# Seven block products in place of eight for the second network's gate and value projections

## The chip, the cores and the metric

The kernel runs on one core of a Trainium2 chip. The core has five engines with a queue each: TensorE (PE in the profile, with its weight loads as PEld), VectorE (DVE), ScalarE (ACT), GpSimd (POOL) and SyncE (SP), which here only issues DMAs. Each engine works through its instructions in their order and waits on semaphores for the others. The metric is the device time of one execution in microseconds: a median of 1072.18 us over three runs (1070.48 to 1072.44).

## The reference, cut to what matters

Linear attention over 4 x 8 heads of 576 positions feeds two dense networks, one after the other, on 2304 tokens of width 512. All values are float32.

```python
x = attention(q, k, v, w_phi)          # [2304, 512] after the heads are joined
h = x @ w_in                           # first network: 512 -> 2048
x = (np.maximum(h, 0.0) ** 2) @ w_out  # 2048 -> 512
gate = 1.0 / (1.0 + np.exp(-(x @ w_gate)))   # second network: 512 -> 1536
val = x @ w_val                              # 512 -> 1536
out = (gate * val) @ w_out2                  # 1536 -> 512
```

## The kernel before, in words

Every matmul operand is kept as two float32r tiles, the rounded value ("hi") and what is left of it ("lo"). A product of two operands is three matmuls, hi x hi, hi x lo and lo x hi (`passes`, L45), summed in PSUM. So each weight tile must be split before use: `wsplit` (L121) takes a raw 128 x 512 float32 tile `wf`, copies hi on ACT (L124) and subtracts lo on DVE or POOL (L125) into a tile `hl`, of which there are six.

The program has three stages: attention, the first network in steps `h_step` and `o_step`, and the second network in steps `gv_step` and `o2_step`. During attention and the first network, `converts` brings every weight into its final form (`weight`, L97 to L110) and parks it in DRAM; a fetch on SP's queue brings it back as `wf` before each use (ten buffers), so that each weight is fetched and split again for every token block.

The second network takes the 2304 tokens in four blocks of 512 and a last one of 256, and for each block the 1536 hidden units in 12 chunks of 128. The step of one chunk (`gv_step`, L536): `project` (L459) makes the gate's 12 matmuls (four contraction tiles, three passes) and the value's 12, each of 512 columns, into one PSUM bank each; ACT takes the sigmoid (L540), DVE multiplies (L541), `g_split` makes the operand `g` (cast on DVE L93, subtraction on DVE L94). `o2_step` (L556) adds the chunk's 12 matmuls into the four banks that hold the block's output, one step later. At the end of a block the banks are copied out in halves by ACT (L575) and DVE (L573). At the start of a block `xsplit` makes hi and lo of its tokens, the tiles `xs`.

PSUM has eight banks, all of one pool (`bank`). The order on each engine comes from a scheduler that runs when the program is built: it puts instructions in the order of the code's priorities as far as its own estimate of when their operands and buffers are free allows, so an engine's order is fixed before the program runs and can interleave two steps.

Of the kernel before, what the change touches and what calls it, by code (L numbers as in the profile page):

```python
# [9 lines left out]
F32 = mybir.dt.float32  # L10
# [9 lines left out]
def attention_moe_moe2(ctx, tc, q, k, v, w_phi, w_in, w_out, w_gate, w_val, w_out2, out):  # L20
    nc = tc.nc
# [35 lines left out]
    def bank(n):  # L57
        return ps.tile([P, 512], F32, tag="a", name="a")[:, :n]
# [72 lines left out]

    def w2_src(n):
        c, o = divmod(n, 3)
        return row_src(w_out2, c) if o == 2 else col_src(w_val if o else w_gate, c)

    nblk = len(blocks)
    ng = len(GROUPS)
# [4 lines left out]


    def pieces_of(s):
        if s < ns1:
            t, c = divmod(s, C1)
            return [((t, 2 * c), 2 * c)], ((t, 2 * c + 1), 2 * c + 1)
        t, c = divmod(s - ns1, C2)
        return [((ng + t, 3 * c + o), NW1 + 3 * c + o) for o in range(2)], ((ng + t, 3 * c + 2), NW1 + 3 * c + 2)

    ahead = 2
    fetched = {}

    def fetch_for(s):
        if s < ns1 + ns2:
            ins, out = pieces_of(s)
            for key, n in [*ins, out]:
                t = wf.tile([P, NJ * P], F32, tag="wf", name="wf")
                nc.sync.dma_start(out=t, in_=parked[n])
                fetched[key] = t  # L160

    def split_in(s):
        if s < ns1 + ns2:
            for key, n in pieces_of(s)[0]:
                if key not in ws:
                    wsplit(key, fetched.pop(key), nc.gpsimd if s < C1 else nc.vector)

    def split_out(s):
        key, n = pieces_of(s)[1]
        wsplit(key, fetched.pop(key), nc.gpsimd if s < ns1 else nc.vector)  # L170

    with ExitStack() as actx:
        cst = actx.enter_context(tc.tile_pool(name="cst", bufs=1))
# [270 lines left out]
                split_in(0)  # L444

    gp = ctx.enter_context(tc.tile_pool(name="gp", bufs=2, reuse_waits="tile"))

    gs = {}
    ys = {}
    last_g = [None]  # L450

    def convert(n):
        park(n, weight(wpa, w1_src(n) if n < NW1 else w2_src(n - NW1)))

    def xsplit(key, t, c0, n):
        for j in range(NJ):
            xsplit_j(key, t, c0, n, j, nc.scalar)

    def project(w, key, t, n):  # L459
        pp = bank(n)  # L460
        k = 0
        for j in range(NJ):
            for x, y in passes:
                nc.tensor.matmul(pp, lhsT=w[:, x, j, :], rhs=xs[key, t, j][:, y, :], start=k == 0, stop=k == 3 * NJ - 1)  # L464
                k += 1
        return pp

    def g_split(key, r):
        g = gp.tile([P, 2, r.shape[1]], F32R, tag="g", name="g", bufs=3)
        last_g[0] = split(g, r)  # L470
        gs[key] = g

    def h_step(g, c):
        w = ws.pop((g, 2 * c))
        for t in GROUPS[g]:
            n = sizes[t]
            pp = project(w, 1, t, n)
            r = gp.tile([P, n], F32, tag="r", name="r")
# [41 lines left out]
    fetch_for(1)  # L520
    for s in range(ns1 + 1):
        if s < ns1:
            t, c = divmod(s, C1)
            if c == 0 and t:
                for u in GROUPS[t]:
                    xsplit(1, u, *blocks[u])
            fetch_for(s + ahead)
            h_step(t, c)
            split_out(s)
            split_in(s + 1)  # L530
        if s >= 1:
            o_step(*divmod(s - 1, C1))
        if s < ns1:
            converts(s)

    def gv_step(t, c):  # L536
        n = sizes2[t]
        pt = [project(ws.pop((ng + t, 3 * c + o)), 2, t, n) for o in range(2)]
        r = gp.tile([P, n], F32, tag="r", name="r2")
        nc.scalar.activation(r, pt[0], AF.Sigmoid)  # L540
        nc.vector.tensor_tensor(r, pt[1], r, ALU.mult)  # L541
        g_split((2, t, c), r)

    def pieces(c0, n):
        c = c0
        while c < c0 + n:
# [9 lines left out]
    def o2_step(t, c):  # L556
        ntt = sizes2[t] // P
        if c == 0:
            os_[t] = [bank(512) for u in range(ntt)]
        w = ws.pop((ng + t, 3 * c + 2))  # L560
        g = gs.pop((2, t, c))
        for u in range(ntt):
            for n, (x, y) in enumerate(passes):
                nc.tensor.matmul(os_[t][u], lhsT=g[:, x, u * P:(u + 1) * P],  # L564
                                 rhs=w[:, y].rearrange("p j f -> p (j f)"),
                                 start=c == 0 and n == 0, stop=c == C2 - 1 and n == 2)
        if c == C2 - 1:
            for u in range(ntt):
                o = gp.tile([P, DM], F32, tag="o", name="osb", bufs=4)
# [9 lines left out]
    done = 0  # L579
    for s in range(ns2 + 2):  # L580
        if s < ns2:
            t, c = divmod(s, C2)
            if c == 0:
                xsplit(2, t, *blocks2[t])
            fetch_for(ns1 + s + ahead)
            gv_step(t, c)
            split_out(ns1 + s)
            split_in(ns1 + s + 1)

        while done < ns2 and done <= s - (1 if s < ns2 - 1 else 2):  # L590
            o2_step(*divmod(done, C2))
            done += 1


# [28 lines left out]
```

## Time and profile before

| what | us |
|---|---|
| median of three runs | 1072.18 |
| the profiled execution's own time | 1071.14 |
| its span, first to last instruction | 1069.3 |
| PE busy | 1052.0 (98%) |
| DVE busy | 705.8 (66%) |
| ACT busy | 516.2 (48%) |
| POOL busy | 218.3 (20%) |

The profiled execution is one run of the program; its own time is 1.84 us above its span, for what lies around the span. Busy time counts the instructions of an engine. Matmuls overlap each other, so the distance between starts, and not the length of one, tells what a matmul costs; the chain in order of time gives these distances.

### The profile page before, as it was taken

How to read it: one execution, taken by the hardware profiler on the slowest of the kernel's cores; microseconds unless marked ns; L12 is line 12 of the kernel's file. 1: busy time of each engine (PE TensorE's matmuls, PEld its weight loads, DVE VectorE, ACT ScalarE, POOL GpSimd, SP SyncE). 2: the span in 40 equal slices, each digit the busy share in tenths (PEclk: the TensorE clock that was granted, in tenths of full speed). 3: DMA queues.
4: the chain of work that ended last, by engine and by line, in shares of the span. 5: the costliest groups of instructions: out<-in, count | busy, mean ns of one | idle time of the engine just before them, and what ended most of it. 6: DMA issues, size and time to landing. Idle time of an engine off the chain costs nothing.

```text
span 1069.3 us, 16941 instructions
## 1 busy us (share of the span) xinstructions
PE 1052.0 (98%) x6128; PEld 833.2 (78%) x6128; DVE 705.8 (66%) x1246; ACT 516.2 (48%) x1044; POOL 218.3 (20%) x278
## 2 busy tenths in 40 slices
PE   8999999799999999999999999999999999999997
PEld 7666665588888888888888888888888888888897
DVE  6899997699754787877978554454445445544574
ACT  7888888244445455554645533242224223323353
POOL 4655655533322222222222000000000000000000
PEclk9999999999999999999999999999999999999999
DMA  9345523176672666766665333333334333433371
GB/s 247 110 148 156 145 62 129 40 239 211 232 251 63 217 206 193 218 195 212 218 207 174 103 99 99 89 119 109 97 90 137 89 99 89 138 93 95 102 216 37
DMA packets 98740, 154.27 MB, mean 144 GB/s; under 512 B 12768, under 2 KB 44640, under 8 KB 98656
## 3 DMA queue, kind: packets, MB, share of 16 engines
q1 hardware_dynamic: 98496, 153.13, 47.9%
q8 instruction: 48, 0.79, 0.3%
q14 instruction: 36, 0.29, 0.1%
q10 hardware_dynamic: 160, 0.07, 0.0%
HBM read 130.61 MB, written 22.54 MB: 143 GB/s over the span
## 4 chain that ended last, share of the span: by engine, by line
PE 90%; DVE 5%; ACT 2%; POOL 1%; issue 0%; DMA 0%; SPq 0%; DVEq 0%; POOLq 0%; ACTq 0%
PE a L464 47%; PE a L497 19%; PE a L564 14%; PE a L319 3%; PE a L356 2%; PE a L293 1%; PE a L326 1%; PE a L349 1%; POOL rc L370 1%; POOL hl L125 1%; PE a L272 1%; PE a L251 1%; DVE km L298 1%; PE a L336 1%; DVE ph L299 1%
## 5 line engine op out<-in xcount | busy, mean ns | idle before, releaser
L464 PE MATMUL a<-xs,hl 128*128 128x512 f32 (+1 forms) x2400 | 527.0, 373 | 2.2 <-DVE xs L93 2.2
L464 PEld LDWEIGHTS a<-xs,hl 128*128 128x128 f32 x2400 | 420.6, 188 | 91.8 <-DVE xs L93 2.4
L124 ACT ACTIVATE hl<-wf 128x512 fp32r<-128x512 f32 x308 | 193.5, 629 | 298.0 <-PE a L564 100.7
L125 DVE TENSOR_TENSOR hl<-wf,hl 128x512 fp32r<-128x512 f32 x228 | 157.1, 690 | 185.7 <-ACT hl L124 180.2
L497 PE MATMUL a<-g,hl 128*128 128x512 f32 (+1 forms) x960 | 215.1, 375 | 2.8 <-DVE g L93 2.3
L497 PEld LDWEIGHTS a<-g,hl 128*128 128x128 f32 x960 | 169.5, 189 | 39.1 <-DVE g L93 2.5
L125 POOL TENSOR_TENSOR hl<-wf,hl 128x512 fp32r<-128x512 f32 x80 | 109.5, 1371 | 296.3 <-ACT hl L124 242.8
L564 PE MATMUL a<-hl,g 128*128 128x512 f32 x648 | 161.1, 396 | 0.0
L564 PEld LDWEIGHTS a<-hl,g 128*128 128x128 f32 x648 | 121.0, 188 | 28.5
L93 DVE CAST g<-r 128x512 fp32r<-128x512 f32 (+1 forms) x140 | 84.2, 601 | 65.0 <-ACT r L480 54.5
L94 DVE TENSOR_TENSOR g<-r,g 128x512 fp32r<-128x512 f32 (+1 forms) x140 | 95.8, 684 | 4.4
L540 ACT ACTIVATE r<-a 128x512 f32<-128x512 f32 (+1 forms) x60 | 33.4, 556 | 117.4 <-PE a L464 117.4
L277 POOL PARTITION_ALL_REDUCE m<-qe x64 | 82.0, 1351 | 29.5 <-ACT qe L275 27.8
L541 DVE TENSOR_TENSOR r<-a,r 128x512 f32<-128x512 f32 (+1 forms) x60 | 38.2, 636 | 56.7 <-PE a L464 56.7
L108 ACT ACTIVATE st<-st 128x512 f32<-128x512 f32 x68 | 46.3, 689 | 46.6 <-DVE w L105 46.4
L479 ACT ACTIVATE r<-a 128x512 f32<-128x512 f32 x80 | 44.0, 552 | 39.0 <-PE a L464 36.1
L105 DVE SCALAR_TENSOR_TENSOR w<-st,w 128x512 uint32<-128x512 uint32 x68 | 51.5, 764 | 1.2
L106 DVE SCALAR_TENSOR_TENSOR w<-st,w 128x512 uint32<-128x512 uint32 x68 | 50.2, 745 | 1.3
L109 DVE SCALAR_TENSOR_TENSOR w<-st,w 128x512 f32<-128x512 f32 x68 | 48.1, 714 | 1.5
L480 ACT ACTIVATE r<-r 128x512 f32<-128x512 f32 x80 | 46.5, 582 | 0.5
L104 DVE TENSOR_SCALAR w<-st 128x512 uint32<-128x512 uint32 x68 | 35.7, 529 | 3.6 <-DMA st<-in_moe_w_out_dram 1.9
L370 POOL COPY rc<-rd 32x9 f32<-32x9 f32 x128 | 26.2, 205 | 49.1 <-DVE rd L363 44.3
(73 smaller groups left out, 732.2 us busy)
## 6 DMA issues: line engine op xcount, KB each, us to landing
wf<-wd SPq DMA_DIRECT2D x308, 256.0 KB, 2.8
wd<-w SPq DMA_DIRECT2D x68, 256.0 KB, 2.8
st<-in_moe_w_out_dram SPq DMA_DIRECT2D x28, 512.0 KB, 4.6
st<-in_moe_w_in_dram SPq DMA_DIRECT2D x16, 512.0 KB, 4.2
st<-in_moe_w_gate_dram SPq DMA_DIRECT2D x12, 512.0 KB, 4.9
st<-in_moe_w_val_dram SPq DMA_DIRECT2D x12, 512.0 KB, 5.5
q<-in_q_dram SPq DMA_DIRECT2D x16, 288.0 KB, 3.9
k<-in_k_dram SPq DMA_DIRECT2D x16, 256.0 KB, 4.2
```

Source lines behind the costliest of these rows:

```text
L93: hi_eng.tensor_copy(dst[:, 0], src)
L94: return nc.vector.tensor_tensor(dst[:, 1], src, f(dst[:, 0]), ALU.subtract)
L105: nc.vector.scalar_tensor_tensor(b, hi, 0xC0000000, b, ALU.bitwise_and, ALU.bitwise_or)
L106: nc.vector.scalar_tensor_tensor(b, lo, 29, b, ALU.logical_shift_right, ALU.bitwise_or)
L109: nc.vector.scalar_tensor_tensor(a, h, TINY, a, ALU.is_ge, ALU.mult)
L124: nc.scalar.activation(d[:, 0], a, AF.Copy)
L125: eng.tensor_tensor(d[:, 1], a, f(d[:, 0]), ALU.subtract)
L277: nc.gpsimd.partition_all_reduce(m, a[:, 1, :], channels=P, reduce_op=bass_isa.ReduceOp.absmax)
L464: nc.tensor.matmul(pp, lhsT=w[:, x, j, :], rhs=xs[key, t, j][:, y, :], start=k == 0, stop=k == 3 * NJ - 1)
L480: nc.scalar.activation(r, r, AF.Square)
L497: nc.tensor.matmul(ys[t][j], lhsT=w[:, x, j, :], rhs=a[:, y, :], start=c == 0 and k == 0 and j % m == 0, stop=c == C1 - 1 and k == 2, skip ...
L564: nc.tensor.matmul(os_[t][u], lhsT=g[:, x, u * P:(u + 1) * P], rhs=w[:, y].rearrange("p j f -> p (j f)"), start=c == 0 and n == 0, stop=c ...
```

## The change

In the four blocks of 512 tokens, two neighbouring chunks (2p and 2p+1) are now computed together. Their weights, gate beside value, are seen as a 2 x 2 matrix of blocks (chunk by contraction half of 256), the tokens as a 2 x 2 matrix of blocks (contraction half by token half of 256). The product of two such matrices is formed with Winograd's form of Strassen's scheme: seven block products in place of eight. A block product (`product`) is 12 matmuls of 256 columns: gate and value, two contraction tiles, three passes. Four of the seven use sums of weight blocks (`s1` to `s4`), made by POOL once per pair and kept in DRAM beside the plain blocks; four use differences of token blocks (`T1` to `T4`), made by DVE once per block in `xsums`. Products that share terms are left in one bank (`X`) and copied out in between by ACT (`keep`, into `kp`), and DVE adds a kept copy to another bank (`joined`, into `cj`). Each of the seven products takes its own weight tile, 256 KB, fetched and split as before; the output network's weights are split on POOL in place of DVE. The last block of 256 tokens keeps its two projections. `run_ahead` fetches 14 tiles and splits 6 tiles ahead of use.

```diff
+    gvd = [dr.tile([P, 2, NJ * P], F32, tag=f"gv{c}", name="gvd") for c in range(C2)]
+    smd = [dr.tile([P, 4, 2, HF], F32, tag=f"sm{p}", name="smd") for p in range(C2 // 2)]
+    def convert2(k):
+        c, o = order2[k]
...
+        a = weight(wpa, col_src(w_val if o else w_gate, c))
+        nc.sync.dma_start(out=gvd[c][:, o], in_=a)
...
+        a11, a12 = kept[o][:, :HF], kept.pop(o)[:, HF:]
+        a21, a22 = a[:, :HF], a[:, HF:]
+        t = sp.tile([P, 4, HF], F32, tag="s", name="s")
+        eng = nc.gpsimd.tensor_tensor
+        eng(t[:, 0], a21, a22, ALU.add)
+        eng(t[:, 1], t[:, 0], a11, ALU.subtract)
+        eng(t[:, 2], a11, a21, ALU.subtract)
+        eng(t[:, 3], a12, t[:, 1], ALU.subtract)
+        nc.sync.dma_start(out=smd[c // 2][:, :, o], in_=t)
...
-        g = gp.tile([P, 2, r.shape[1]], F32R, tag="g", name="g", bufs=3)
+        g = gp.tile([P, 2, r.shape[1]], F32R, tag="g", name="g", bufs=4)
...
+    def xsums(t):
...
+        direct("B11", 0, 0)
+        direct("B21", 1, 0)
+        t1 = total("T1", sub_(h[0, 1], h[0, 0]))
+        t2 = total("T2", sub_(h[1, 1], lambda kt: t1[:, kt]))
+        split(operand("T2"), t2, nc.scalar)
+        t3 = total("T3", sub_(h[1, 1], h[0, 1]))
+        split(operand("T3"), t3, nc.scalar)
+        split(operand("T1"), t1, nc.scalar)
+        direct("B22", 1, 1)
+        t4 = total("T4", sub_(h[1, 0], lambda kt: t2[:, kt]))
+        split(operand("T4"), t4, nc.scalar)
...
+    def product(b, key, x, t, start):
+        w, v = take(key), xs[x, t]
+        for m in range(2):
+            k = 0
+            for kt in range(2):
+                for i, j in passes:
+                    nc.tensor.matmul(b[:, m * HF:(m + 1) * HF], lhsT=w[:, i, 2 * m + kt, :], rhs=v[:, j, kt, :],
+                                     start=start and m == 0 and k == 0, stop=k == 5, skip_group_check=True)
+                    k += 1
+    def keep(name):
+        side[name] = gp.tile([P, 2 * HF], F32, tag="kp", name="kp", bufs=3)
+        nc.scalar.activation(side[name], acc["X"], AF.Copy)
+    def joined(name, b):
+        c = gp.tile([P, 2 * HF], F32, tag="cj", name="cj", bufs=3)
+        nc.vector.tensor_tensor(c, side[name], acc[b], ALU.add)
...
+    def p1(t, p):
+        acc["X"] = bank(512)
+        product(acc["X"], ("a11", t, p), "B11", t, True)
+        keep("p1")
+    def p2(t, p):
+        acc["Z"] = bank(512)
+        product(acc["Z"], ("a12", t, p), "B21", t, True)
+        gated(t, 2 * p, 0, joined("p1", "Z"))
+    def p6(t, p):
+        product(acc["X"], ("s2", t, p), "T2", t, False)
+        keep("u2")
+    def p7(t, p):
+        acc["Y"] = bank(512)
+        product(acc["Y"], ("s3", t, p), "T3", t, True)
+    def p5(t, p):
+        product(acc["X"], ("s1", t, p), "T1", t, False)
+        keep("u4")
+        gated(t, 2 * p + 1, 1, joined("u4", "Y"))
+    def p3(t, p):
+        product(acc["X"], ("s4", t, p), "B22", t, False)
+        gated(t, 2 * p, 1, acc["X"])
+    def p4(t, p):
+        product(acc["Y"], ("a22", t, p), "T4", t, False)
+        gated(t, 2 * p + 1, 0, joined("u2", "Y"))
...
+                for f_, k in ((p1, "a11"), (p2, "a12"), (p6, "s2"), (p7, "s3"), (p5, "s1"), (None, 0),
+                              (p3, "s4"), (p4, "a22"), (None, 0)):
+                    if f_ is None:
+                        out_act()
...
+                    if f_ is p5 and p == pairs - 1:
+                        act(xsums, t + 1)
...
+            wsplit(key, fetched.pop(key), nc.gpsimd if key[0] == "out" else nc.vector)
...
-    for s in range(ns2 + 2):
...
+    for k, what in enumerate(acts):
+        run_ahead(first[k], 14, 6)
+        what[0](*what[1:])
```

In the rows of order that follow, `a` is a PSUM bank, `hl` a split weight, `xs` and `xq` split token operands, `xt` a token difference, `u` the raw tokens and `osb` an output tile.

On PE, early in the second network's first block, the order before was:

```order
L564 MATMUL a<-hl,g 128x512 x4
L464 MATMUL a<-xs,hl 128x512 x23
L564 MATMUL a<-hl,g 128x512 x12
L464 MATMUL a<-xs,hl 128x512 x24
L564 MATMUL a<-hl,g 128x512 x12
L464 MATMUL a<-xs,hl 128x512 x24
```

In the changed program PE's order shortly after the start of a block of 512 tokens, a pair and its neighbours, is:

```order
L642 MATMUL a<-xq,hl 128x256 x18
L642 MATMUL a<-xs,hl 128x256 x12
L568 MATMUL a<-hl,g 128x512 x2
L642 MATMUL a<-xq,hl 128x256 x12
L568 MATMUL a<-hl,g 128x512 x18
L642 MATMUL a<-xs,hl 128x256 x12
L568 MATMUL a<-hl,g 128x512 x4
L642 MATMUL a<-xq,hl 128x256 x18
L642 MATMUL a<-xs,hl 128x256 x24
L642 MATMUL a<-xq,hl 128x256 x18
L642 MATMUL a<-xs,hl 128x256 x12
```

The runs of 24 matmuls of 512 columns are gone; products of 12 matmuls of 256 columns follow each other in ones and twos, and the output's matmuls stand between them in pieces of 2, 4 and 18.

On DVE, where one block of 512 tokens gives way to the next, the order before was:

```order
L94 TENSOR_TENSOR g<-r_7692,g 128x512
L125 TENSOR_TENSOR hl<-wf,hl 128x512 x2
L94 TENSOR_TENSOR xs<-u,xs 128x256 x4
L541 TENSOR_TENSOR r_7751<-a,r_7751 128x512
L94 TENSOR_TENSOR xs<-u,xs 128x256 x4
L93 CAST g<-r_7751 128x512
L125 TENSOR_TENSOR hl<-wf,hl 128x512
L94 TENSOR_TENSOR g<-r_7751,g 128x512
L125 TENSOR_TENSOR hl<-wf,hl 128x512
L541 TENSOR_TENSOR r_7830<-a,r_7830 128x512
```

In the changed program the densest part of that place is:

```order
L95 TENSOR_TENSOR xs<-xt,xs 128x512
L95 TENSOR_TENSOR g<-r_8007,g 128x512
L127 TENSOR_TENSOR hl<-wf,hl 128x512
L95 TENSOR_TENSOR xq<-u,xq 128x256
L617 TENSOR_TENSOR xt<-u,xt 128x256 x2
L95 TENSOR_TENSOR xq<-u,xq 128x256
L127 TENSOR_TENSOR hl<-wf,hl 128x512
L617 TENSOR_TENSOR xt<-u 128x256 x2
L652 TENSOR_TENSOR cj<-kp,a 128x512
L95 TENSOR_TENSOR xs<-xt,xs 128x512
L127 TENSOR_TENSOR hl<-wf,hl 128x512
L660 TENSOR_TENSOR r_8191<-cj,r_8191 128x256
```

Before, eight subtractions of 256 columns stand among the ordinary work of two steps; now the token differences (`xt`) and the splits of seven operands (`xq`, `xs`) stand among weight splits, gate products and the additions into `cj`.

## Rows read from the trace of the kernel before

**Rows 1.** The page's first line and its part 1, busy time of each engine.

```profile
span 1069.3 us, 16941 instructions
...
PE 1052.0 (98%) x6128; PEld 833.2 (78%) x6128; DVE 705.8 (66%) x1246; ACT 516.2 (48%) x1044; POOL 218.3 (20%) x278
```

**Rows 2.** The page's part 2, busy tenths in 40 slices of the span.

```profile
PE   8999999799999999999999999999999999999997
...
DVE  6899997699754787877978554454445445544574
```

**Rows 3.** Chain in order of time: start us, duration us, engine, tile, line, count.

```profile
715.51 5.14 PE a L464 x22
...
816.60 5.14 PE a L464 x22
...
1019.77 2.82 PE a L464 x24
...
1057.77 2.84 PE a L464 x24
```

**Rows 4.** Windows: stretch, length, then busy us (instructions) by engine, granted clock, DMA.

```profile
400.00:500.00 100.00, 100.00 (x429) 80.38 (x428) 77.75 (x114) 51.92 (x94) 23.55 (x18) 1.00 0.67 207
...
500.00:600.00 100.00, 100.00 (x428) 80.40 (x427) 79.17 (x115) 53.55 (x95) 23.62 (x17) 1.00 0.61 189
...
640.00:740.00 100.00, 100.00 (x429) 80.42 (x428) 48.51 (x84) 31.71 (x59) 0.00 (x0) 1.00 0.36 103
```

**Rows 5.** Groups by form, DVE: shapes, count, busy us, mean ns, idle before.

```profile
L125 DVE TENSOR_TENSOR hl<-wf,hl 128x512 fp32r<-128x512 f32 x228 | 157.1, 690 | 185.7 <-ACT hl L124 180.2 <-DMA wf<-wd 3.0 <-DMA st<-in_moe_w_gate_dram 0.8
...
L541 DVE TENSOR_TENSOR r<-a,r 128x512 f32<-128x512 f32 x48 | 33.2, 691 | 53.7 <-PE a L464 53.7
...
L94 DVE TENSOR_TENSOR xs<-u,xs 128x256 fp32r<-128x256 f32 x32 | 11.8, 416 | 1.5 <-ACT xs L91 1.5
...
L541 DVE TENSOR_TENSOR r<-a,r 128x256 f32<-128x256 f32 x12 | 5.0, 418 | 3.0 <-PE a L464 3.0
...
L573 DVE COPY osb<-a 128x256 f32<-128x256 f32 x18 | 6.9, 415 | 2.0 <-ACT osb L575 2.0
```

**Rows 6.** Groups by form, ACT.

```profile
L124 ACT ACTIVATE hl<-wf 128x512 fp32r<-128x512 f32 x308 | 193.5, 629 | 298.0 <-PE a L564 100.7 <-issue 84.2 <-PE a L464 74.5
...
L502 ACT ACTIVATE u<-a 128x512 f32<-128x512 f32 x16 | 8.6, 603 | 0.8 <-PE a L497 0.8
...
L540 ACT ACTIVATE r<-a 128x256 f32<-128x256 f32 x12 | 4.6, 386 | 11.6 <-PE a L464 11.6
```

**Rows 7.** Timeline of the second network: start us, duration us, engine, line.

```profile
1001.29 5.78 PE L464 MATMUL a<-xs,hl 128*128 128x512 f32 x24
...
1004.30 0.60 ACT L540 ACTIVATE r<-a 128x512 f32<-128x512 f32 x1 [2.18 <-PE a L464]
...
1008.38 0.42 DVE L93 CAST g<-r 128x512 fp32r<-128x512 f32 x1
...
1008.84 0.69 DVE L94 TENSOR_TENSOR g<-r,g 128x512 fp32r<-128x512 f32 x1
```

**Rows 8.** Windows of line 93 alone (the cast of g).

```profile
500.00:600.00 100.00, 15.72 (x18) 1.00 0.61 189
...
640.00:740.00 100.00, 5.04 (x12) 1.00 0.36 103
```

**Rows 9.** Timeline of the first network, POOL and DVE.

```profile
542.13 1.29 POOL L125 TENSOR_TENSOR hl<-wf,hl 128x512 fp32r<-128x512 f32 x1 [4.20 <-ACT hl L124]
...
542.60 1.10 DVE L93 CAST g<-r 128x512 fp32r<-128x512 f32 x1 [1.54 <-ACT r L480]
```

**Rows 10.** Groups by form, POOL.

```profile
L125 POOL TENSOR_TENSOR hl<-wf,hl 128x512 fp32r<-128x512 f32 x80 | 109.5, 1371 | 296.3 <-ACT hl L124 242.8 <-DMA wf<-wd 31.5 <-PE a L497 10.9
```

**Rows 11.** DMA issues: KB each, median us from issue to landing.

```profile
wf<-wd SPq DMA_DIRECT2D x308, 256.0 KB, 2.8
...
st<-in_moe_w_gate_dram SPq DMA_DIRECT2D x12, 512.0 KB, 4.9
```

More of the change, by code (lines that the diff above doesn't have):

```diff
@@ L518, in converts @@
                 nc1 += 1
[L520 to L542, printed above, removed]
     def pieces(c0, n):
@@ L559, in o2_step @@
             os_[t] = [bank(512) for u in range(ntt)]
-        w = ws.pop((ng + t, 3 * c + 2))
+        w = take(("out", t, c))
         g = gs.pop((2, t, c))
@@ L577, in o2_step @@
                     nc.sync.dma_start(out=dst, in_=o[po:po + m, :])
-    done = 0
-    for s in range(ns2 + 2):
[L581 to L592, printed above, removed]
+    pairs = C2 // 2
@@ new lines, in half, with operand, direct, total @@
+    def half(t, d, j, kt):
+        c0 = blocks2[t][0] + j * HF
+        (_, _, u, o), = cols(c0, HF)
+        return xy[u, 2 * d + kt][:, o:o + HF]
+    def xsums(t):
+        if sizes2[t] < 2 * HF:
+            xsplit(2, t, *blocks2[t])
+            return
+        def operand(k):
+            if k in ("B11", "B21", "T2"):
+                a = xq.tile([P, 2, 2, HF], F32R, tag="xq", name="xq")
+            else:
+                a = xp.tile([P, 2, 2, HF], F32R, tag=f"xs{('T3', 'T1', 'B22', 'T4').index(k)}_512", name="xs")
+            xs[k, t] = a
+            return a
+        def direct(k, d, j):
+            a = operand(k)
+            for kt in range(2):
+                split(a[:, :, kt], half(t, d, j, kt), nc.scalar)
+        def total(k, fill):
+            b = xq.tile([P, 2, HF], F32, tag="xt", name="xt", bufs=3)
+            for kt in range(2):
+                fill(b[:, kt], kt)
+            return b
+        def sub_(x, y):
+            return lambda dst, kt: nc.vector.tensor_tensor(dst, x(kt), y(kt), ALU.subtract)
+        h = {(d, j): (lambda kt, d=d, j=j: half(t, d, j, kt)) for d in range(2) for j in range(2)}
+        direct("B11", 0, 0)
[9 more added lines that the diff above has]
+        split(operand("T4"), t4, nc.scalar)
@@ new lines, in p3, with gv_step @@
+    def p3(t, p):
[4 more added lines that the diff above has]
+        gated(t, 2 * p + 1, 0, joined("u2", "Y"))
+    def gv_step(t, c):
+        n = sizes2[t]
+        pt = [project(take((o, t, c)), 2, t, n) for o in ("gate", "val")]
+        r = gp.tile([P, n], F32, tag="r", name="r2", bufs=3)
+        nc.scalar.activation(r, pt[0], AF.Sigmoid)
+        nc.vector.tensor_tensor(r, pt[1], r, ALU.mult)
+        g_split((2, t, c), r)
@@ new lines, in sources, with act @@
+    def sources(t, p):
+        return {"a11": gvd[2 * p][:, :, :HF], "a12": gvd[2 * p][:, :, HF:], "a22": gvd[2 * p + 1][:, :, HF:],
+                "s1": smd[p][:, 0].rearrange("p m f -> p (m f)"), "s2": smd[p][:, 1].rearrange("p m f -> p (m f)"),
+                "s3": smd[p][:, 2].rearrange("p m f -> p (m f)"), "s4": smd[p][:, 3].rearrange("p m f -> p (m f)")}
+    acts = []
+    first = []
+    seq = []
+    pend = []
+    def act(f, *args, need=()):
+        first.append(len(seq))
+        seq.extend(need)
+        acts.append((f, *args))
@@ new lines, in out_act @@
+    def out_act():
+        if pend:
+            t, c = pend.pop(0)
+            act(o2_step, t, c, need=[(("out", t, c), lambda: parked["out", c])])
+    for t, n in enumerate(sizes2):
+        if n == 2 * HF:
+            for p in range(pairs):
+                for f_, k in ((p1, "a11"), (p2, "a12"), (p6, "s2"), (p7, "s3"), (p5, "s1"), (None, 0),
+                              (p3, "s4"), (p4, "a22"), (None, 0)):
+                    if f_ is None:
+                        out_act()
+                    else:
+                        act(f_, t, p, need=[((k, t, p), lambda k=k, t=t, p=p: sources(t, p)[k])])
+                    if f_ is p5 and p == pairs - 1:
+                        act(xsums, t + 1)
+                pend += [(t, 2 * p), (t, 2 * p + 1)]
+        else:
+            for c in range(C2):
+                act(gv_step, t, c, need=[((o, t, c), lambda i=i, c=c: gvd[c][:, i])
+                                         for i, o in enumerate(("gate", "val"))])
+                pend.append((t, c))
+                while len(pend) > 1:
+                    out_act()
@@ new lines, in attention_moe_moe2, with run_ahead, take @@
+    out_act()
+    done_f = done_s = 0
+    def run_ahead(k, nf, nsp):
+        nonlocal done_f, done_s
+        while done_f < min(len(seq), k + nf):
+            fetch(seq[done_f][0], seq[done_f][1]())
+            done_f += 1
+        while done_s < min(len(seq), k + nsp):
+            key = seq[done_s][0]
+            wsplit(key, fetched.pop(key), nc.gpsimd if key[0] == "out" else nc.vector)
+            done_s += 1
+    def take(key):
+        return ws.pop(key)
+    fetch_for(1)
+    for s in range(ns1 + 1):
+        if s < ns1:
+            t, c = divmod(s, C1)
+            if c == 0 and t:
+                for u in GROUPS[t]:
+                    xsplit(1, u, *blocks[u])
+            fetch_for(s + ahead)
+            h_step(t, c)
+            split_out(s)
+            split_in(s + 1)
+        if s == ns1 - 3:
+            xsums(0)
+        if s >= ns1 - 2:
+            run_ahead(3 * (s - ns1 + 2), 10, 0 if s < ns1 else 4)
+        if s >= 1:
+            o_step(*divmod(s - 1, C1))
+        if s < ns1:
+            converts(s)
```

70 lines of the change are left out of this document (47 added, 23 removed).

## The prediction

> **What bounds the kernel now.** I read four views. The busy times first: PE is busy for 98% of a span of 1069.3 us, DVE for 66%, ACT and POOL for less [rows 1]. Then the slices: PE's digit is 9 in nearly all of them once attention is past [rows 2], so the question is whether PE runs at its pace or only looks busy. The windows answer it: each 100 us of either network hold 428 or 429 matmuls of 512 columns, whatever the other engines do, at a granted clock of 1.00 (2.4 GHz) [rows 4]. The reader is to see that DVE at 79% with POOL at 24% leaves PE as undisturbed as DVE at 49% with POOL idle. The chain in order of time gives the price of a matmul. Two block starts lie 816.60 - 715.51 = 101.09 us apart; a block is 12 steps of 36 matmuls, 432 in all, so 234.0 ns each. In the last block, with 256 columns, nine steps take 1057.77 - 1019.77 = 38.00 us, 4.222 us each; less the six output matmuls of 512 columns (1.404 us) this leaves 2.818 us for 24 matmuls, 117.4 ns each, with a fresh weight load every time [rows 3]. Half the columns cost half the time. PE bounds the second network, so what is taken from PE comes off the time unless another engine or a handoff takes its place.
>
> **What PE loses.** A pair of chunks on 512 tokens takes 48 matmuls of 512 columns now, 48 x 234.0 = 11.23 us, and 7 x 12 = 84 of 256 columns after, 84 x 117.4 = 9.86 us. That is 1.37 us less; six pairs in four blocks are 24 pairs, 32.9 us. With its 24 output matmuls (5.62 us) a pair goes from 16.85 to 15.48 us, a block from 101.1 to 92.9 us.
> The Trainium skill, in "TensorE: Matmul & The Clock Gate", section "Wait — 56ns, not 53.3ns?", speaks against shorter matmuls: each carries about 2.5 ns that do not shrink with its columns. By that, 36 more matmuls in each of 24 pairs would give back 2.2 us, an estimate from the page's figure. The trace differs: two at 117.4 ns are 0.8 ns more than one at 234.0, at most 0.7 us in all; the row decides, and 117.4 holds it already.
>
> **What DVE gets.** Per pair of 15.48 us: seven weight splits of 0.690; three additions of a bank to a kept copy, for which the row of a PSUM and an SBUF operand stands, 0.691; four gate products of 256 columns, 0.418 [rows 5]; two splits of g, each a cast of 0.42 and a subtraction of 0.69 where POOL rests [rows 7]. That is 4.83 + 2.07 + 1.67 + 2.22 = 10.8 us, 70%. Per block come the token operands: eight differences and six low halves of 256 columns at 0.416 and four low halves of 512 at 0.69, 8.6 us, and four output copies at 0.415, 1.7 us [rows 5, 7]. A block has 75 us of DVE work for 92.9 us of PE, 81%; the first network ran at 78 to 79% without one matmul lost [rows 4]. So in the mean it is hidden. At a block change it is not: there a pair carries 10.8 + 8.6 + 1.7 = 21.1 us for 15.5 us of PE, 5.6 us too many, as the order on DVE shows. Weights are split up to five tiles ahead, some 8 us of PE work, which takes up part of it. Bounds are 0 and 5.6 us at each change; I take 1.5, since the changes before cost PE nothing with a smaller heap of the same kind (the step of 101.09 us contains one, and 432 x 234 is all of it). Three changes of this kind and the crossing from the first network, where ACT also copies that network's last outputs, make four: 6 us, between 0 and 22.
>
> **What ACT gets.** Per pair nine weight copies of 0.629, three kept copies (the nearest row is a bank copied out, 0.603) and four sigmoids of 0.386 [rows 6]: 9.0 us, 58%. The load is hidden by PE; the handoffs may not be. Bank X is used by four products in a row, and each next one waits for ACT's copy. From the rows: 12 matmuls that began at 1001.29 end at about 1004.10, ACT starts at 1004.30 [rows 7], so 0.2 us; then 0.6 us of copy; how long PE takes to see it no row shows, between 0 and another 0.2 us. About 0.9 us, while one other product on PE covers 1.41. A weight copy in front on ACT (0.629) makes it 1.5, so a wait of 0 to 0.6 us at each of two handoffs per pair; the third has 2.81 us of output matmuls over it. PE's order shows other products and pieces of output put into these places. I take 0.1 us per pair, 2.4 us, near the lower end, since the first network's interleaved order lost nothing [rows 4]; the upper end is 48 x 0.6 = 29 us. Three banks for X, Y and Z beside the output's four leave one spare, so a pair's first product need not wait for the pair before.
>
> **What POOL and the queues get.** POOL, idle in the second network [rows 4], splits 12 output weights per block at 1.371 us [rows 10], 16.5 of 92.9 us. It also forms 48 weight sums of 256 columns in the first network, about half of 1.371 each by size, 33 us over some 300. They stand between its splits, whose tiles are asked for a step (5.6 us) later. What they do to DVE: the cast of g takes 5.04/12 = 0.42 us with POOL idle and 15.72/18 = 0.87 with POOL at work [rows 8]; in one place 1.10 us beside a POOL split [rows 9]. At 0.45 us per cast and 12 casts a block DVE rises by 5.4 us to 80.4, 87%: still hidden, with less left for block changes. In the first network 48 x 0.45 = 22 us spread over 300 us would take DVE from 79 to 86%, hidden as well; if that cover were gone, no more than POOL's 33 us. SP's queue carries nine tiles of 256 KB per pair, 2.36 MB in 15.5 us or 152 GB/s, less than the 189 to 207 GB/s of the first network [rows 4]. The halves of plain blocks are read in shorter runs; 2.8 us to landing now, 4.9 for the strided loads of raw weights [rows 11], against ten fetch buffers or some 12 us. The store of weight sums waits on SP's queue for POOL, with fetches behind it that are two steps early. I cost all of this at nothing, 0 to 5 us.
>
> **The sum.** From the profiled execution's own 1071.14 us: -32.9 + 6 + 2.4 = 1046.6 us. The median of the three runs is 1.0 us above that execution, so 1047.6; I say 1047.
>
> **Rivals.**
> Handoffs decide (A). The order on PE is fixed before the run; wherever a product is put exactly behind an expected copy, lateness is a stall, and a pair has five or more such places against none in the plain order before. For it: the pieces of 2, 4 and 18 matmuls on PE. Against: the first network's pieces cost nothing. At 0.35 us for each of 48 bank handoffs, 17 us in place of 2.4: 1062.
> DVE becomes the bound through POOL (B). If each POOL split held DVE up for its whole 1.371 us, a block would have 75 + 16.5 = 91.5 us of DVE work on 92.9 of PE, no slack, and each block change would cost the whole 5.6 us: 22 in place of 6, so 1063. The Trainium skill, "SBUF — State Buffer", section "SBUF: two separate sides", would have it so: DVE and GpSimd share a port pair by an exclusive lock, also for DVE operations with two SBUF inputs. The trace agrees for the cast, but the weight split, with two SBUF inputs, keeps a mean of 0.690 us over both networks.
> Slower than before (C). The ring of six split weight tiles: a tile is freed when its product ends, and its refill takes 0.2 + 0.629 + 0.690 us, about 1.5, now against 1.41 us of a product where it was 2.81. If products pulled forward fill the ring, refills stand in line and PE waits at nearly every one of 9 x 24 = 216 tiles. It decides from (32.9 - 6) / 216 = 0.125 us per tile; at 0.2 us it costs 43 us: 1071.14 - 32.9 + 6 + 43 + 1 = 1088. Against it: six tiles are 10 us of work for a refill of 1.5.
> No gain at all (D): were a 256-column matmul over 11.23 / 84 = 133.7 ns in half banks, the saving would be gone: about 1080 with the stalls. The last block's nine steps speak against it.
>
> **How the numbers follow.** Chances: the forecast 0.60 (1040 to 1055 by itself), A 0.17, B 0.13, C 0.07, D 0.03. With no stall at all the time is 1071.14 - 32.9 + 1 = 1039. The range goes from 1037 to 1064: it holds the forecast, and B and most of A; what is left out is C, D and the far end of A, under 0.2. About 0.2% (2 us) can be told from no change. Faster needs less than 31 us of stalls: the forecast, B and most of A, 0.90; within 0.2%, 0.02; slower, 0.08.
>
> **What would show it.** Right: 24 matmuls of 256 columns in about 2.82 us in the second network's first four blocks; a block near 93 to 95 us; PE waits of a microsecond or two at block changes, on DVE's `xq`, `xs` or weight splits; DVE near 85%. A would show as many PE waits below 0.6 us on the copies `kp`; B as DVE without idle time through a whole block, with casts and subtractions over 1 us; C as PE waits on `hl` all through; D as more than 117 ns per matmul without any wait. Longer time in the first network, where PE's order is nearly the same, would prove the cover there wrong.

## The result, and the profile after

| | before | after |
|---|---|---|
| median, us | 1072.31 (1070.48 to 1073.58, 4 runs) | 1042.12 (1040.69 to 1044.65, 4 runs) |
| the profiled execution's own time | 1071.14 | 1042.41 |
| its span | 1069.3 | 1040.6 |

The ratio after to before is 0.9722, interval 0.9699 to 0.9746. The forecast was 1047 us, range 1037 to 1064.

The page after, its first line, its busy times and PE's slices (answering to [rows 1, 2]):

```profile
span 1040.6 us, 19417 instructions
...
PE 1022.2 (98%) x6992; PEld 855.5 (82%) x6992; DVE 831.9 (80%) x1422; ACT 600.9 (58%) x1248; POOL 359.0 (34%) x386
...
PE   8999999899999999999999999999999999999997
...
DVE  6899999489864888898898877788769768967753
```

PE is as full as before and is busy for 29.8 us less. DVE has gone from 66 to 80%, ACT from 48 to 58% and POOL from 20 to 34%; PE's slices show no gap for it.

The windows after (answering to [rows 4]; length, busy us and instructions of PE, PEld, DVE, ACT and POOL, granted clock, DMA):

```profile
400.00:500.00 100.00, 99.66 (x426) 79.83 (x425) 87.74 (x115) 52.39 (x94) 45.64 (x40) 1.00 0.73 230
500.00:600.00 100.00, 100.00 (x428) 80.40 (x427) 86.83 (x113) 51.98 (x94) 39.41 (x34) 1.00 0.69 218
...
640.00:740.00 100.00, 98.72 (x683) 91.31 (x683) 79.69 (x135) 56.34 (x115) 19.98 (x13) 1.00 0.52 161
740.00:840.00 100.00, 100.00 (x698) 92.91 (x696) 79.11 (x138) 57.03 (x117) 18.91 (x12) 1.00 0.52 164
840.00:940.00 100.00, 100.00 (x702) 93.12 (x701) 80.21 (x130) 57.03 (x115) 20.07 (x14) 1.00 0.53 164
```

In the second network (from 640 on) a stretch holds about 700 matmuls of the two lengths; each of the three has a block change in it, and only the first has PE below 100. In the first network, 426 matmuls stand where 429 stood, with DVE at 88% for 78.

The chain of work in order of time (answering to [rows 3]), the piece behind the first network's last matmul, one whole pair with the piece behind it in three blocks, and the last projections:

```profile
614.28 11.39 PE a L642 x96
...
662.26 9.86 PE a L642 x84
672.11 1.87 PE a L568 x8
...
766.79 1.87 PE a L568 x8
...
859.85 1.87 PE a L568 x8
...
1029.15 2.82 PE a L492 x24
```

The seven products of a pair, run without a break, take 9.86 us, the forecast's figure: 117.4 ns a matmul. Same places of two blocks lie 859.85 - 766.79 = 93.06 us apart (forecast without stalls 92.9), and 766.79 - 672.11 = 94.68 us where the block change held PE up. PE's waits in the two networks that add up to over a microsecond (engine, line, waited for: us in total, times, longest):

```profile
PE a L525 <- DVE g L94: 2.4, 2, 2.0
PE a L492 <- DVE xs L94: 2.1, 1, 2.1
...
PE a L568 <- DVE g L94: 1.3, 1, 1.3
```

The first two belong to the first network; the last is the only wait in the second network. The timeline around it (start us, us, engine, line; in brackets what it waited, and for what):

```profile
715.92 0.38 ACT L579 ACTIVATE osb<-a 128x256 f32<-128x256 f32 x1 [1.97 <-DMA out_dram<-osb]
716.20 0.62 ACT L126 ACTIVATE hl<-wf 128x512 fp32r<-128x512 f32 x1
...
716.90 1.31 POOL L127 TENSOR_TENSOR hl<-wf,hl 128x512 fp32r<-128x512 f32 x1 [12.55 <-ACT hl L126]
...
717.28 1.48 DVE L95 TENSOR_TENSOR g<-r,g 128x512 fp32r<-128x512 f32 x1
...
719.25 1.29 POOL L127 TENSOR_TENSOR hl<-wf,hl 128x512 fp32r<-128x512 f32 x1 [1.04 <-ACT hl L126]
719.28 2.42 DVE L127 TENSOR_TENSOR hl<-wf,hl 128x512 fp32r<-128x512 f32 x2
...
722.29 0.41 DVE L94 CAST g<-r 128x512 fp32r<-128x512 f32 x1
...
722.85 2.10 PE L568 MATMUL a<-hl,g 128*128 128x512 f32 x8 [1.28 <-DVE g L94]
```

ACT's fourth output copy waits 1.97 us for one of three output tiles, which an output DMA still reads (the kernel before has four, `bufs=4`; the change made them three); weight copies and bank copies stand behind it on ACT. DVE, which waits for those, then meets two POOL splits: its subtraction of 0.69 us takes 1.48 beside the first, and a pair of them 2.42 beside the second. The first ends 0.55 us after POOL's end (717.28 + 1.48 against 716.90 + 1.31), the pair 1.16 us after it: as if DVE had begun when POOL stopped. The cast of `g` then comes 1.28 us late for PE.

The sum in the traces: from the last matmul of the first network, which ends at 614.28, to the end of the last projection at 1029.15 + 2.82 are 417.7 us. The work in it is 422.2 us (24 pairs of 15.48 and 12 steps of 4.222), less 4.2 for the 36 matmuls of 256 columns that stand before 614.28 (8, 2, 20 and 6 in the chain) and 2.8 for the 12 output matmuls that follow the last projection: 415.2. So the second network loses 2.5 us. The spans differ by 28.7 us = 32.9 - 2.5 - 1.7; the 1.7 is what attention and the first network take longer.

### The profile page after: what moved, and what is told of

It is laid out like the page before. It is cut to its first block, busy times and chain, and to the rows that moved or that the text cites. A ratio compares the mean times of both kernels' runs of the same rounds, so it can differ in the third digit from the quotient of the medians.

```text
span 1040.6 us, 19417 instructions
## 1 busy us (share of the span) xinstructions
PE 1022.2 (98%) x6992; PEld 855.5 (82%) x6992; DVE 831.9 (80%) x1422; ACT 600.9 (58%) x1248; POOL 359.0 (34%) x386
## 4 chain that ended last, share of the span: by engine, by line
PE 88%; DVE 6%; ACT 2%; POOL 2%; DMA 1%; issue 1%; SPq 0%; DVEq 0%; ACTq 0%; POOLq 0%
PE a L642 22%; PE a L492 22%; PE a L525 19%; PE a L568 14%; PE a L342 3%; PE a L379 2%; PE a L316 2%; PE a L349 1%; PE a L372 1%; POOL rc L393 1%; POOL hl L127 1%; PE a L295 1%; PE a L274 1%; DVE km L321 1%; DMA kr<-in_k_dram 1%
## 5 line engine op out<-in xcount | busy, mean ns | idle before, releaser
L127 POOL TENSOR_TENSOR hl<-wf,hl 128x512 fp32r<-128x512 f32 x140 | 207.7, 1485 | 547.8 <-ACT hl L126 454.7
L126 ACT ACTIVATE hl<-wf 128x512 fp32r<-128x512 f32 x380 | 236.6, 628 | 149.5 <-issue 55.7
L492 PE MATMUL a<-xs,hl 128*128 128x512 f32 (+1 forms) x1248 | 251.9, 353 | 2.1 <-DVE xs L94 2.1
L492 PEld LDWEIGHTS a<-xs,hl 128*128 128x128 f32 x1248 | 205.6, 189 | 39.5 <-DVE xs L94 2.3
L642 PE MATMUL a<-xs,hl 128*128 128x256 f32 x1152 | 147.5, 280 | 0.0
L642 PEld LDWEIGHTS a<-xs,hl 128*128 128x128 f32 x1152 | 142.8, 188 | 2.5
L642 PE MATMUL a<-xq,hl 128*128 128x256 f32 x864 | 114.3, 280 | 0.0
L642 PEld LDWEIGHTS a<-xq,hl 128*128 128x128 f32 x864 | 110.0, 188 | 3.7
L648 ACT ACTIVATE kp<-a 128x512 f32<-128x512 f32 x72 | 42.7, 593 | 50.1 <-PE a L642 49.8
L652 DVE TENSOR_TENSOR cj<-kp,a 128x512 f32<-128x512 f32 x72 | 48.5, 681 | 16.3 <-ACT kp L648 16.1
L106 DVE SCALAR_TENSOR_TENSOR w<-st,w 128x512 uint32<-128x512 uint32 x68 | 53.0, 787 | 1.1
```

Source lines behind the costliest of these rows:

```text
L106: nc.vector.scalar_tensor_tensor(b, hi, 0xC0000000, b, ALU.bitwise_and, ALU.bitwise_or)
L642: nc.tensor.matmul(b[:, m * HF:(m + 1) * HF], lhsT=w[:, i, 2 * m + kt, :], rhs=v[:, j, kt, :], start=start and m == 0 and k == 0, stop=k = ...
L652: nc.vector.tensor_tensor(c, side[name], acc[b], ALU.add)
```

## The experiments

Each variant's order was made anew by the scheduler, so it differs from its parent in more places than its edit. Ratios are to the kernel before, run on the same chip; the changed kernel's is 0.9722.

| run | what | median us | ratio and interval |
|---|---|---|---|
| e1_eighth | an eighth product | 1074.46 | 1.0027, 1.0013 to 1.0041 |
| e2_pool_alone | the kernel before, output weights split on POOL | 1070.27 | 0.9995, 0.9986 to 1.0004 |
| e3_osb4 | four output tiles | 1041.06 | 0.9722, 0.9705 to 0.9738 |
| e4_out_dve | output weights split on DVE | 1039.69 | 0.9711, 0.9698 to 0.9725 |
| e5_dve_more | 33 us more on DVE | 1045.03 | 0.9761, 0.9743 to 0.9780 |
| e6_keep_twice | 43 us more on ACT | 1044.43 | 0.9753, 0.9739 to 0.9766 |
| e7_128 | products in 128 columns | 1252.89 | 1.1700, 1.1684 to 1.1716 |
| e8_no_sums | no weight sums | 1040.20 | 0.9716, 0.9702 to 0.9729 |
| e9_both | e3 and e4 | 1040.54 | 0.9715, 0.9701 to 0.9730 |
| e10_sums_dve | e9, sums on DVE | 1040.07 | 0.9709, 0.9694 to 0.9723 |
| e11_ring5 | five weight tiles | 1046.08 | 0.9768, 0.9752 to 0.9784 |

**Is the gain the missing product?** The first run gives it back, and keeps all the rest of the scheme:

```diff
-        for m in range(2):
+        for again, m in ((a, m) for a in range(2 if key[0] == "a12" else 1) for m in range(2)):
```

> The changed kernel with one of its seven products (a12 with B21) made twice in every pair, the second time anew over the first: an eighth block product, and nothing else on ACT, DVE, POOL or the queues. Theory (PE bounds both kernels, and the gain is the count of matmuls): 24 pairs x 12 matmuls x 117.4 ns = 33.8 us come back, 1042 + 34 = 1076 us, 1072 to 1077 if the longer pairs hide what stalls there were; ratio to the kernel before 1.000 to 1.005. Rival (the gain lies in the other edits, or another engine bounds the changed kernel): under 15 us are added, 1057 or less.

It took 1074.46 us, 32.3 above the changed kernel: 24 x 12 matmuls at 117.4 ns are 33.8. A stretch of its second network:

```profile
640.00:740.00 100.00, 100.00 (x710) 93.44 (x710) 74.92 (x129) 53.16 (x109) 19.58 (x12) 1.00 0.52 154
```

PE is full, and the block product is worth its matmuls and little else. It lands 3.0 us above the kernel before (1.4 to 4.4 by the interval); 96 matmuls of 117.4 ns for 48 of 234.0 in 24 pairs are 0.9 of that, and the rest was not told apart.

The second run does one of those parts alone in the kernel before, the split of output weights on POOL:

```diff
-        wsplit(key, fetched.pop(key), nc.gpsimd if s < ns1 else nc.vector)
+        wsplit(key, fetched.pop(key), nc.gpsimd)
```

> The kernel before with one part of the change alone: the output weights of the second network are split on POOL in place of DVE. Theory (PE bounds, DVE has room, the place of the split is nothing): 1072 us, ratio 0.998 to 1.002, with DVE's share in the second network down from 48% to about 40%. Rival (the moved split is part of the gain): 1065 us or less. Rival (POOL holds DVE up for its whole instruction and PE waits): 1076 us or more.

0.9995: no part of the gain. Its stretch from 640 to 740 has 429 matmuls, as before, with DVE at 41% for 48.5.

**What made the wait at the block change?** A fourth output tile, and apart from it the output weights' splits back on DVE:

```diff
-                o = gp.tile([P, DM], F32, tag="o", name="osb", bufs=3)
+                o = gp.tile([P, DM], F32, tag="o", name="osb", bufs=4)
```

> The changed kernel with four output tiles in place of three, as before the change. In its trace the fourth output copy of a block waits on ACT for an output DMA to land (2.0 us at the first block change, 716 us), and PE then waits 1.3 us once. Theory (that wait is the only stall left in the second network): ACT's wait for output DMAs is gone, PE's wait of 1.3 us too, 1040 to 1041.5 us, ratio 0.970 to 0.972. Rival (the stall is DVE's load at the block change): 1042 to 1043, with the wait of PE still there.

```diff
-            wsplit(key, fetched.pop(key), nc.gpsimd if key[0] == "out" else nc.vector)
+            wsplit(key, fetched.pop(key), nc.vector)
```

> The changed kernel with the output weights' splits back on DVE, POOL idle in the second network. DVE gains 12 x 0.69 = 8.3 us of work per block and loses what POOL holds up; in the run with 33 us more DVE work the time rose by about 4 us. Theory (DVE is close to PE's pace at the block changes, so its load shows a little): 1043 to 1046 us, ratio 0.973 to 0.976. Rival (POOL's splits are what hold DVE up, by their whole length): faster than the changed kernel, 1039 to 1041, ratio 0.969 to 0.971.

Either one alone removes PE's wait. With four tiles ACT no longer waits for an output DMA, and the stretch measured above takes 416.1 us for 417.7; with the splits on DVE it takes 416.1 as well, although ACT still waits for output DMAs there (four times, 4.2 us in all, 1.2 at most). So in these runs the wait needed both: ACT held by the output tile, and POOL in DVE's way. The 0.9 us left over 415.2 stand in no wait. In the median neither can be told from the changed kernel. My expectation of the second was wrong: 12 more operations on DVE in each block did not make it later. The profile says why. One block of the changed kernel, DVE's groups by form (count, busy us, mean ns, idle before):

```profile
L127 DVE TENSOR_TENSOR hl<-wf,hl 128x512 fp32r<-128x512 f32 x42 | 29.5, 711 | 8.4 <-DMA wf<-gvd 4.2 <-ACT hl L126 3.9
L660 DVE TENSOR_TENSOR r<-cj,r 128x256 f32<-128x256 f32 x19 | 13.2, 697 | 0.2
...
L95 DVE TENSOR_TENSOR g<-r,g 128x512 fp32r<-128x512 f32 x12 | 12.0, 1000 | 0.1
L94 DVE CAST g<-r 128x512 fp32r<-128x512 f32 x12 | 5.7, 479 | 0.2
L660 DVE TENSOR_TENSOR r<-a,r 128x256 f32<-128x256 f32 x6 | 2.5, 424 | 5.8 <-ACT r L659 5.8
```

The same place of the kernel with the splits on DVE, POOL idle:

```profile
L127 DVE TENSOR_TENSOR hl<-wf,hl 128x512 fp32r<-128x512 f32 x55 | 37.0, 686 | 8.4 <-ACT hl L126 7.2 <-DMA wf<-gvd 0.7
...
L95 DVE TENSOR_TENSOR g<-r,g 128x512 fp32r<-128x512 f32 x12 | 8.2, 686 | 0.1
L660 DVE TENSOR_TENSOR r<-cj,r 128x256 f32<-128x256 f32 x18 | 7.5, 418 | 0.0
L94 DVE CAST g<-r 128x512 fp32r<-128x512 f32 x12 | 5.1, 424 | 0.2
L660 DVE TENSOR_TENSOR r<-a,r 128x256 f32<-128x256 f32 x6 | 2.5, 424 | 10.4 <-ACT r L659 10.4
```

The gate product from `cj`, two inputs in SBUF, takes 697 ns beside POOL and 418 without; the same product with one input in PSUM takes 424 in both. The subtraction of `g` takes 1000 and 686. The three groups with two SBUF inputs lose 19 x 0.279 + 12 x 0.314 + 42 x 0.025 = 10.1 us in a block, the casts another 0.7: 10.8 us for POOL's 12 splits, 0.9 us each. (The block before it, compared in the same way, gives some 9 us, 0.75 each.) Done on DVE itself a split costs 0.69 at most. Moving it to POOL gave DVE more to do. Why the weight splits, which have two SBUF inputs as well, lose so little is not shown.

**Both together, and the weight sums.** The first network has fewer matmuls in a stretch where POOL makes weight sums. One run leaves the sums out and stores plain blocks in their places:

```diff
-        eng(t[:, 0], a21, a22, ALU.add)
...
-        nc.sync.dma_start(out=smd[c // 2][:, :, o], in_=t)
+        for i, b in enumerate((a21, a22, a11, a12)):
+            nc.sync.dma_start(out=smd[c // 2][:, i, o], in_=b)
```

> The changed kernel without the 48 weight sums on POOL: plain blocks are stored in their places, so four of the seven products have wrong weights. Theory (the sums cost the first network a little through DVE: 426 matmuls between 400 and 500 us against 429 before): that stretch has 428 or 429 again, DVE falls there from 88% to about 78%, and the time by 0.5 to 1.5 us, ratio 0.971 to 0.972. Rival (the sums are hidden and the loss is the queue of stores): 426 as now, ratio 0.972 or more.

Its stretch that answers to the first of the windows after:

```profile
400.00:500.00 100.00, 100.00 (x428) 80.40 (x427) 77.77 (x113) 52.43 (x93) 24.60 (x18) 1.00 0.76 236
```

Two of the three matmuls are back, half a microsecond, and DVE is back from 87.7 to 77.8%. So the sums on POOL cost the first network that much in this stretch. The rest of its 1.7 us lies outside it (below).

Two more runs join both remedies, and then put the sums on DVE:

```diff
-                o = gp.tile([P, DM], F32, tag="o", name="osb", bufs=3)
+                o = gp.tile([P, DM], F32, tag="o", name="osb", bufs=4)
...
-            wsplit(key, fetched.pop(key), nc.gpsimd if key[0] == "out" else nc.vector)
+            wsplit(key, fetched.pop(key), nc.vector)
```

> The changed kernel with four output tiles and with the output weights split on DVE, POOL idle in the second network. Each alone left no PE wait in the second network and made it about 1.6 us shorter in its trace. Theory (both took away the same wait): together no more than each, 1039 to 1041 us, ratio 0.970 to 0.972. Rival (two separate losses): another 1 to 2 us, ratio 0.969 or less.

```diff
-        eng = nc.gpsimd.tensor_tensor
+        eng = nc.vector.tensor_tensor
```

> As the run with both, and the 48 weight sums of the first network made on DVE in place of POOL. Without the sums the stretch from 400 to 500 us had 428 matmuls in place of 426. Theory (POOL's sums hold DVE up longer than DVE itself needs for them): DVE's share from 400 to 600 us falls from 87% to 80 to 85%, 427 or 428 matmuls there, 0.3 to 1 us less than the run with both. Rival (it is the work of the sums, wherever it is done): 426 matmuls or fewer, no gain or a loss up to 2 us.

With both, the stretch takes 416.0 us: each remedy removed the same wait, so they do not add. With the sums on DVE the stretch from 400 to 500 has 429 matmuls again (the next 100 us 427, for 428 with both remedies), with DVE at 86.3% and POOL at 24.1: DVE's share came down less than expected. At 0.9709 this and e4 are the best of the versions run, but their intervals overlap the changed kernel's; I do not call them faster.

**How much slack is left?** Two additions in SBUF per pair on DVE, whose results nothing uses:

```diff
     def p7(t, p):
+        for _ in range(2):
+            e = gp.tile([P, 2 * HF], F32, tag="ex", name="ex", bufs=1)
+            nc.vector.tensor_tensor(e, side["p1"], side["p1"], ALU.add)
```

> The changed kernel with two more DVE additions of 512 columns in each pair (their results are not used): 24 x 2 x 0.69 = 33 us more DVE work in 372 us, from some 80 to 89% there. Theory (DVE has room up to PE's pace): 0 to 4 us more, 1042 to 1046, ratio 0.972 to 0.976. Rival (DVE is near its bound through POOL, order and handoffs, so that added work shows): 10 to 33 us more, 1052 to 1075.

And every kept copy of bank X made twice on ACT:

```diff
-        nc.scalar.activation(side[name], acc["X"], AF.Copy)
+        for _ in range(2):
+            nc.scalar.activation(side[name], acc["X"], AF.Copy)
```

> The changed kernel with each of the 72 copies of bank X into kp made twice on ACT: each handoff from one product on X to the next is 0.6 us longer, ACT has 43 us more work of 372, from 57 to some 68%. Theory (other products and output pieces stand in between, and the order is made anew around it): 0 to 6 us more, 1042 to 1048, ratio 0.972 to 0.978. Rival (the handoffs decide): 0.3 to 0.6 us at 48 or 72 places, 14 to 43 us more, 1056 or above.

33 us of work on DVE (48 additions of 0.69) cost 3 to 4 us, 43 us on ACT (72 copies of 0.59) 2 to 3. PE's waits in the second network, the first kernel's and then the second's:

```profile
PE a L642 <- ACT kp L648: 1.3, 3, 0.7
PE a L642 <- ACT hl L126: 0.9, 2, 0.5
```

```profile
PE a L642 <- ACT kp L649: 1.0, 1, 1.0
PE a L642 <- ACT hl L126: 0.7, 1, 0.7
PE a L642 <- DVE hl L127: 0.4, 2, 0.2
```

With every copy 0.6 us longer, PE waits once for a copy, not at 48 places. The handoffs of bank X have slack, and rival A falls. DVE at 85% begins to tell, by a tenth of what is added. (Both intervals touch the changed kernel's, 0.9743 to 0.9780 and 0.9739 to 0.9766 against 0.9699 to 0.9746, so that these few us are uncertain.)

**The ring of split weights**, rival C, with one tile fewer:

```diff
-                hlp = ctx.enter_context(tc.tile_pool(name="hlp", bufs=6, side="right", reuse_waits="tile"))
+                hlp = ctx.enter_context(tc.tile_pool(name="hlp", bufs=5, side="right", reuse_waits="tile"))
```

The pool serves both networks.

> The changed kernel with five split weight tiles in the ring in place of six, in both networks. Theory (six tiles are 10 us of PE work for a refill of 1.5 us, so one fewer is hidden): 0 to 4 us more, 1042 to 1046, ratio 0.972 to 0.976. Rival (the ring is what PE would wait for next, 0.1 us or more at each of 216 tiles): 20 us or more, 1062.

1046.08 us, some 4 to 5 more, with these waits in the second network and no others:

```profile
PE a L568 <- POOL hl L127: 4.5, 3, 2.0
```

Three waits for the splits that POOL makes, not 216 for every tile. A wait can cost more than its length: after one of the two of 2.0 us PE's granted clock was 1.2 GHz for a time (0.91 in the mean from 680 to 700 us), after the other it stayed at 1.00, 2.4 GHz. In the first network the stretch from 400 to 500 has 422 matmuls for 426. A little over what I expected; far from rival C.

**Is the half-length matmul still priced by its columns?** Each matmul of a product cut into two of 128 columns:

```diff
-                    nc.tensor.matmul(b[:, m * HF:(m + 1) * HF], lhsT=w[:, i, 2 * m + kt, :], rhs=v[:, j, kt, :],
-                                     start=start and m == 0 and k == 0, stop=k == 5, skip_group_check=True)
+                    for e in range(0, HF, P):
+                        nc.tensor.matmul(b[:, m * HF + e:m * HF + e + P], lhsT=w[:, i, 2 * m + kt, :],
+                                         rhs=v[:, j, kt, e:e + P], start=start and m == 0 and k == 0 and e == 0,
+                                         stop=k == 5, skip_group_check=True)
```

> The changed kernel with each matmul of the seven products cut into two of 128 columns, each with its own weight load: the same columns, 24 x 84 = 2016 more matmuls. Theory (cost goes with columns down to here): 58.7 ns each, 1042 to 1046 us. Rival (a fixed cost of each matmul, or the weight load sets a floor; the nearest row, matmuls of 128 columns in attention at 85 ns each): 24 x 168 x 26 ns = 106 us more, 1148.

Both expectations missed. The chain, and one stretch:

```profile
648.72 16.03 PE a L643 x144
```

```profile
700.00:800.00 100.00, 100.00 (x794) 95.68 (x794) 55.60 (x98) 40.59 (x80) 10.75 (x8) 1.00 0.36 109
```

16.03 / 144 = 111.3 ns a matmul, for 117.4 with twice the columns: 24 x 84 x (2 x 111.3 - 117.4) ns = 212 us, and the median rose by 211. PE waits for nothing, and its weight loads are busy 96% of the time (93% in the changed kernel, 80% before). So halving the 256 columns saves 6 ns of 117, and no more. The rival expected had the right kind of cost but misread its row: the matmuls that start some 83 ns apart in attention are transposes of 96 columns. Transposes of 128 columns, each with a weight load of its own, start 109 ns apart in the trace before, and by that row the rival's sum would have been 203 us more. The Trainium skill, "TensorE: Matmul & The Clock Gate", section "LDWEIGHTS (loading the stationary operand)", gives a load 1/1.2 ns per weight column, which makes 106.7 ns for 128, an estimate from its figure. The 111.3 measured would fit a bound by weight loads; but the transposes of 96 columns load 128 weight columns each, and start 83 ns apart all the same, in threes. Whether the load or another cost of each matmul sets the 111.3 was not told apart: no run kept the load out.

## Why the prediction was right, point by point

- **PE's saving, -32.9 us: right.** 24 matmuls of 256 columns take 2.82 us (9.86 for 84), and one product put back costs 32.3. Rival D (over 133.7 ns) falls.
- **Block changes, +6 (0 to 22): too high.** About 1.6 us. One wait of 1.28 us at the first change, none at the other two or at the crossing, and it was for `g`, not for `xq`, `xs` or a weight split. It came from an output tile, ACT's queue behind it and POOL's splits in DVE's way; the heap of token operands, on which the term was built, did not show. The output tiles were not in my working at all, although their count, cut from four to three, stood in the code.
- **Handoffs of bank X, +2.4 (0 to 29): nothing.** No PE wait on `kp` in the changed kernel, and doubling each copy brought one of 1.0 us. Rival A falls.
- **POOL, the queues and the first network, 0 (0 to 5): 1.7, inside the bounds.** Some 0.6 us is the weight sums on POOL. I had sized a sum at half a split, 0.69 us; the profile after has 0.81 to 1.10. "Hidden as well" at 86% DVE was nearly so: it ran at 87.7% and lost three matmuls of 429. Most of the rest is the clock where the first network starts, which no step of mine touched. Windows of before, then of after, and the same piece of work (the second step's 24 output matmuls) in both chains:

```profile
205.00:210.00 5.00, 2.71 (x14) 2.16 (x15) 2.49 (x4) 2.73 (x6) 2.04 (x2) 1.00 0.15 46
210.00:215.00 5.00, 4.51 (x15) 3.30 (x14) 4.69 (x10) 3.20 (x6) 0.66 (x1) 0.66 0.00 0
...
220.48 4.21 PE a L497 x24
```

```profile
205.00:210.00 5.00, 3.86 (x12) 3.08 (x12) 1.02 (x3) 2.33 (x5) 0.70 (x1) 0.66 0.18 50
210.00:215.00 5.00, 3.60 (x10) 2.55 (x11) 4.77 (x10) 2.31 (x6) 1.86 (x2) 0.69 0.00 0
...
221.59 4.21 PE a L525 x24
```

  PE waits here for the first tokens and the first `g` in both kernels (2.2 and 2.3 us before, 2.1 and 2.0 after). In between its clock falls from 2.4 to 1.2 GHz for a part of 5 us before and of 10 us after, and the same work starts 1.11 us later. With the output splits on DVE the dip is in one window (0.97, then 0.68) and that work starts at 219.72; without weight sums it is in two (0.66, 0.69) and starts at 220.96. So the dip does not go with the sums. From that work to its end the first network takes 0.6 us longer than before, and without the sums as long as before: that is their price.
- **DVE near 87%: it ran at 79 to 80%**, and for two reasons that partly cancel. Each duration in the profile overlaps the next one, so the sum of durations is not the time that DVE needs. Four operations back to back in the changed kernel:

```profile
707.11 0.68 DVE L127 TENSOR_TENSOR hl<-wf,hl 128x512 fp32r<-128x512 f32 x1
707.71 0.68 DVE L95 TENSOR_TENSOR g<-r,g 128x512 fp32r<-128x512 f32 x1
708.31 0.68 DVE L127 TENSOR_TENSOR hl<-wf,hl 128x512 fp32r<-128x512 f32 x1
708.91 0.68 DVE L652 TENSOR_TENSOR cj<-kp,a 128x512 f32<-128x512 f32 x1
```

  They start every 0.60 us and last 0.68. Taken by their starts my sum is over a tenth smaller, as the kernel with POOL idle shows: with its 12 splits more it comes to 83.3 us a block, 90%, and DVE ran at 76 to 78%. Against that, POOL holds DVE up for longer than the 0.45 us per cast that I had taken.
- **Rival B: its mechanism holds, its end does not.** I set the Trainium skill's page "SBUF — State Buffer", section "SBUF: two separate sides", aside because weight splits kept a mean of 0.690 us. That mean was over both networks, in the second of which POOL rested [rows 4], and beside POOL the weight splits are the least hit of all (711 ns for 686). The Trainium skill's rule there is an exclusive lock between GpSimd and a DVE operation with two SBUF inputs. The rows agree for the gate product (697 ns for 418), for the subtraction of `g` (1000 for 686) and for the product with an input in PSUM, which is not held (424 and 424). But a POOL split costs DVE 0.9 us, not its whole 1.371, and DVE's idle 20% took it up.
- **Rival C: falls** with five tiles at +4 to 5 us, where it asked for 43 with six.

In the sum: predicted -32.9 + 6 + 2.4 + 0 = -24.5 for the profiled execution, measured -28.7 in the span. The mis-sized terms are the block changes (4.4 too many) and the handoffs (2.4 too many); against them stand 1.7 for the first network and the 0.9 that the second network loses in no wait. The saving itself was right, and the small terms were off both ways.

Open: what lengthens the dip of the clock at the first network's start (1.1 us of the 1.7). The record points to chance of the execution: the changed kernel's slowest execution (1044.65 us) had a mean granted clock of 0.993, the two fastest (1040.69 and 1041.84) of 0.997. Whether the program's order has a part in it is not shown.

## What to carry to other kernels

When PE is full and waits for nothing, price an algorithm that trades matmuls for additions by the matmul's spacing at its new shape, read from the trace, and then count only what exceeds the slack of the other engines: here 85% busy on DVE and 67% on ACT cost a tenth of what was added or less. Stop at a free size of 256 columns where each float32r matmul loads its own weights: at 128 columns a matmul cost 111.3 ns, nearly as much as the 117.4 at 256. Before such a price is taken from the nearest row, check that row's shape. Before moving a VectorE operation to GpSimd as relief, compare the means of the two-input operations with GpSimd at work and idle; here the move cost VectorE more than it took away.

## What the runs showed of the hardware that was not expected

- At a granted clock of 1.00 a float32r matmul with its own weight load costs 234.0 ns at 512 columns, 117.4 at 256 and 111.3 at 128.
- A GpSimd split of 128x512 (1.45 us in the second network) lengthened DVE's operations by 0.9 us in all in one block; operations with an input in PSUM kept their length. In the timeline above, a DVE operation that met one ended 0.55 us after it.
- GpSimd's four kinds of additions of 128x256 differ, and none costs half of a 128x512 one:

```profile
L155 POOL TENSOR_TENSOR s<-s,w 128x256 f32<-128x256 f32 x12 | 13.2, 1097 | 0.0
L156 POOL TENSOR_TENSOR s<-w 128x256 f32<-128x256 f32 x12 | 10.8, 899 | 0.0
...
L154 POOL TENSOR_TENSOR s<-w 128x256 f32<-128x256 f32 x12 | 9.7, 809 | 41.4 <-DVE w L110 41.4
```
